# Order of the work inside a load, in a decode kernel with cached attention: the spread of P over two loads, its turn in the second, P V ahead of the second scores

## The chip, the cores and the metric

The kernel runs on one core of one Trainium2 chip. The metric is the device time of one execution in microseconds (us), taken as the median of several executions. The profile is one profiled execution on the same core.

## What is computed

One decode step (one new token for each of 8 rows) of a transformer layer: a layer norm, an attention over the last 2048 cached positions, and a mixer with a GELU MLP. Cut to what matters here:

```python
h  = x + A(layernorm(x), k_cache, v_cache, wq, wo)     # attention
h2 = h + B(layernorm(h), w1, w2, w3, w4)               # mixer, MLP

def A(x, k_cache, v_cache, wq, wo):   # 8 rows, 32 query heads, 8 KV heads, Dh = 128
    q = (x @ wq) ...                  # one query per row and head
    k, v = the last W = 2048 of the 8192 cached positions, each KV head shared by 4 heads
    p = softmax(q k^T / sqrt(Dh))
    return (p v) @ wo
```

With a sequence length of 1 the token shift of B leaves only zeros, so `w1` and `w2` are not read. What must be read is K and V (8 rows x 8 heads x 2048 x 128 in bf16, 33.6 MB each) and the weights wq, wo, w3 and w4: 79.18 MB in all.

## The kernel before, in words

**Loads.** K and V are read in 16 loads each, n = 0 to 15. A load holds 4 of the 8 KV heads of one batch row, 2 MiB, so a row b has two loads: the first (even n, in the code `t == 0`) and the second (odd n, `t == 1`). A load of K is worked on in four blocks (`i = 4n` to `4n + 3`). K and V have four buffers each. All large transfers are issued from one queue (SP) in program order: in step n of the loop K of load n, then V of load n - 3, and twice a piece of wo. K waits until K of load n - 4 has been turned, V until P V of four loads earlier is done. At the end V of load 15 comes in four pieces, then the rest of wo, then w3 and w4 into buffers of K.

**Program order.** Every engine has a list of operations written by hand; semaphores tie the lists. The order in which the Python functions are called is the order on each engine, and an engine never passes a waiting operation. The parts of a step:

- `turn_K(i)` (lines 298 to 311): TensorE (PE) transposes one block of K, 8 matmuls of 128x128 (L305), into one of two PSUM buffers `kT_ps`, used in turn; ScalarE (ACT) copies the low half of the result to SBUF (L292), VectorE (DVE) the high half (L293). The buffer is free again for the turn after the next when both copies are done.
- `pe_QK(m)` (L320): the scores of two turned blocks, 8 matmuls with 512 columns, summed in `S_ps`. `pe_QK(2n)` needs blocks 0 and 1 of the load, `pe_QK(2n+1)` blocks 2 and 3.
- `softmax_1`, `_2`, `_3` (second load of a row only): the maximum over the scores (DVE, L330), brought over partitions with a small matmul (L334), a reduction and a negation (DVE), brought back with another (L345), copied (DVE, L348); then the exponential on ACT (L351) into `P_sb`.
- `softmax_spread(b, part)`, part = 0 to 3: P is multiplied with a mask into the wide tile `Pz`, two DVE operations for each part (L366); part 0 also forms the masked row sums (L357).
- `softmax_4(b)`: `Pz` is turned like a block of K, 8 matmuls (L377) into the next `kT_ps`, and copied by ACT and DVE into `pS`, the weights of P V.
- `softmax_5(b)`: the row sums brought over partitions by a matmul into the small PSUM tile `sm` (L385), their reciprocals and a product (DVE, L388 and L394).
- `emit_PVs(k)`: P V in blocks (w = 0 to 3 of a load, 8 matmuls of 256 columns each, L421), three loads behind K (four in the last two steps); after the last block of a load ACT copies the result out (L430, `evict_o`).
- `fold_os` (matmuls L439, and a DVE product L445 into `oK`) and `turn_os` (matmuls L457, a DVE copy L462 into `o2`) finish a load of P V. L439, L457, L385, L334 and L345 all write the tile `sm`, one after the other.

**Order of a step before.** Both loads: turn 0, fold, turn 1, turn 2, first scores, `turn_os`, turn 3, one block of P V, second scores. In a first load the four parts of the spread of the row before lie between the turns, `softmax_5` stands ahead of turn 3, and `softmax_4` after the second scores, followed by three blocks of P V. In a second load `softmax_1` to `_3` follow the second scores, with a block of P V between each, and one behind them.

**After the loop**: the spread of the last row in one go (8 DVE operations), P V of load 12, `softmax_5` and `softmax_4` of the last row, P V of loads 13 to 15 in another form (L411, 16 matmuls a block), the projection with wo (`pe_wo`, L498), the layer norm, w3 (L631), GELU and w4 (L659), and the store.

Of the kernel before, what the change touches and what calls it, by code (L numbers as in the profile page):

```python
# [48 lines left out]
SPR = 4  # L49
# [32 lines left out]
def bass_sequential_preLN__sliding_block_cached__mixer_s_mlp__decode_kernel(  # L82
# [24 lines left out]
    with es:  # L107
# [178 lines left out]
        def turn(mm, dst, waits, waits_hi=(), free=()):  # L286
            k = len(e_Tlo)
            prev = lambda l: l[k - 2] if k >= 2 else None
            ps = kT_ps[k % 2]
            e_Tlo.append(PE.op(lambda e: mm(e, ps, 0), prev(e_lo), e_pk, e_pp, *waits))  # L290
            e_Thi.append(PE.op(lambda e: mm(e, ps, 1), prev(e_hi), *waits_hi))
            e_lo.append(AC.op(lambda e: e.activation(dst[:, 0:1024], ps[:, 0:1024], ACT.Copy), e_Tlo[k], *free))  # L292
            e_hi.append(DV.op(lambda e: e.tensor_single_scalar(dst[:, 1024:2048].bitcast(dt.int32),  # L293
                                                               ps[:, 1024:2048].bitcast(dt.int32), 0, ALU.bitwise_or),
                              e_Thi[k], *free))
            return e_Thi[k], (e_lo[k], e_hi[k])

        def turn_K(i):
            n, u = divmod(i, U)
            src = knat[:, n % NK, 2048 * u:2048 * (u + 1)].bitcast(dt.float32)  # L300

            def mm(e, ps, half):
                ps = ps[:, :].bitcast(dt.float32)
                for c in range(4 * half, 4 * half + 4):
                    ins = e.matmul(ps[:, c * 128:(c + 1) * 128], src[:, c * 128:(c + 1) * 128], perm_k[:, :],  # L305
                                   is_transpose=True)
                return ins
            e_T[i], e_ev[i] = turn(mm, kT_sb[:, i % NKT, :], ((sem_k[n % NK], 16 * (n // NK + 1)),),
                                   free=(e_QK.get((i - NKT) // 2),))

        def pe_QK(m):
            n, v = divmod(m, 2)
            b, t = divmod(n, NU)
            lo = 24 - 16 * t - 8 * v
            kT = kT_sb[:, (2 * m) % NKT:(2 * m) % NKT + 2, :].rearrange("p u (c j r k) -> p j k (u c) r", c=8, j=J, k=2)

            def f(e):
                for k in range(2):
                    for j in range(J):
                        ins = e.matmul(S_ps[b % 2][32 * j:32 * (j + 1), :].rearrange("p (c r) -> p c r", c=16),  # L320
                                       qz[:, b % 2, J * t + j, k, lo:lo + 32], kT[:, j, k],
                                       start=(t == 0 and v == 0 and k == 0), stop=(t == NU - 1 and v == 1 and k == 1),
                                       tile_position=(0, 32 * j), skip_group_check=True)
                return ins
            e_QK[m] = PE.op(f, *e_ev[2 * m], *e_ev[2 * m + 1], e_qw[b], e_qs, e_exp.get(b - 2))
# [29 lines left out]
        def softmax_spread(b, part):  # L355
            if part == 0:
                e_lsel[b] = DV.op(lambda e: e.tensor_scalar(lsel[:, :], sel_f[:, :], lcol[:, b % 2:b % 2 + 1], None,  # L357
                                                            ALU.mult), e_exp[b], e_Lb.get(b - 1), e_sel)
            w = 512 // SPR
            for a in range(w // 64):  # L360
                o = w * part + 64 * a
                p = P_sb[:, o:o + 64]
                p_bc = bass.AP(tensor=p.tensor, offset=p.offset, ap=[p.ap[0], [1, RR], [0, J], [RR, 2]])
                m = mJ[:, :]
                m_bc = bass.AP(tensor=m.tensor, offset=m.offset, ap=[m.ap[0], [0, RR], [1, J], [0, 2]])
                e_Pz[b, part] = DV.op(lambda e, o=o, p_bc=p_bc, m_bc=m_bc: e.tensor_tensor(  # L366
                    Pz[:, 0, J * o:J * (o + 64)].rearrange("p (x j k) -> p x j k", j=J, k=2), p_bc, m_bc, ALU.mult),
                    e_exp[b], e_PT.get(b - 1), e_mJ)

        def softmax_4(b):  # L370
            s = b % 2

            def mm(e, ps, half):
                ps = ps[:, :].bitcast(dt.float32)
                src = Pz[:, 0, :].bitcast(dt.float32)
                for c in range(4 * half, 4 * half + 4):
                    ins = e.matmul(ps[:, c * 128:(c + 1) * 128], src[:, c * 128:(c + 1) * 128], perm_p[:, :],  # L377
                                   is_transpose=True)
                return ins
            e_PT[b], e_pS[b] = turn(mm, pS[:, s, :], (e_Pz[b, SPR // 2 - 1],), (e_Pz[b, SPR - 1],),  # L380
                                    free=(e_PV.get(NU * U * (b - 1) - 1),))
            
        def softmax_5(b):
            s = b % 2
            e_Lb[b] = PE.op(lambda e: e.matmul(sm[:, LB], ones_f[:, :], lsel[:, :], start=True, stop=True),  # L385
                            e_lsel[b], sm_read[0])
            s = b % 2
            e_r = DV.op(lambda e: e.reciprocal(rL[:, s, :].rearrange("p (t j h) -> p t j h", t=NU, j=J),  # L388
                                               sm[:, LB].rearrange("p (j t h) -> p t j h", j=J, t=NU)), e_Lb[b],
                        e_sc.get(NU * (b - 2) + 1))  # L390
            sm_read[0] = e_r
            r_bc = bass.AP(tensor=rL[:, :, :].tensor, offset=s * H, ap=[rL[:, :, :].ap[0], [1, H], [0, R]])
            k_bc = bass.AP(tensor=mK[:, :].tensor, offset=0, ap=[mK[:, :].ap[0], [0, H], [1, R]])
            e_rL[b] = DV.op(lambda e: e.tensor_tensor(rLk[:, s, :, :], r_bc, k_bc, ALU.mult), e_r, e_mK)  # L394
# [56 lines left out]
        def turn_o(n):  # L451
            b, t = divmod(n, NU)
            dst = sm[:, 0:16]

            def f(e):
                for r in range(R):
                    ins = e.matmul(dst[32 * r:32 * (r + 1), :].rearrange("p (g k) -> p g k", k=R), mE[:, :],  # L457
                                   oK[:, n % 2, :, r, :], start=True, stop=True,
                                   tile_position=(0, 32 * r), skip_group_check=True)
                return ins  # L460
            e = PE.op(f, e_mE, e_sc[n], sm_read[0])
            e_scale[n] = DV.op(lambda e: e.tensor_copy(o2[:, J * t:J * (t + 1), :, b],  # L462
                                                       dst.rearrange("p (g k) -> p g k", k=R)), e)
            sm_read[0] = e_scale[n]
# [62 lines left out]
        def turn_os(to):  # L527
            while turned[0] < to:
                turn_o(turned[0])
                turned[0] += 1  # L530

        def emit_PVs(to):
            while pv[0] < min(to, NBLK):
                emit_PV(pv[0])
                pv[0] += 1

        for n in range(NUN):
            if n < NUN - 1:
                load_k(n)
            if n == NUN - 2:  # L540
                load_k(n + 1)
            if n >= LVD:
                load_v(n - LVD)
            if n in WO_AT:
                load_wo(WO_G[WO_AT.index(n)], sem_wo)
            i = U * n
            b, t = divmod(n, NU)
            lag = LVD + (n >= NUN - 2)
            pvs = lambda k: emit_PVs(U * (n - lag) + k)
            if t == 0 and b >= 1:  # L550
                spread = lambda part: softmax_spread(b - 1, part)
            else:
                spread = lambda part: None
            if t == 0:
                fill_q(b)
            turn_K(i)
            spread(0)
            fold_os(pv[0] // U)
            turn_K(i + 1)
            spread(1)  # L560
            turn_K(i + 2)
            spread(2)
            pe_QK(2 * n)
            turn_os(pv[0] // U)
            if t == 0 and b >= 1:
                softmax_5(b - 1)
            turn_K(i + 3)
            spread(3)
            pvs(1)
            pe_QK(2 * n + 1)  # L570
            if t == 0 and b >= 1:
                softmax_4(b - 1)
            if t == 1:
                softmax_1(b)
                pvs(2)
                softmax_2(b)
                pvs(3)
                softmax_3(b)
            pvs(4)
        for part in range(SPR):  # L580
# [127 lines left out]
```

## Time and profile before

| | |
|---|---|
| median of 3 runs | 200.86 us (199.88, 200.86, 203.51) |
| the profiled execution: its own time | 199.77 us |
| its span, first to last instruction | 198.5 us |
| PE busy, weight loads busy | 145.5 us, 112.6 us |
| DVE busy, ACT busy, POOL busy | 101.2 us, 89.5 us, 7.4 us |
| read from HBM | 79.18 MB |
| PE idle for K's transfer (L305) | 1.7 us in 2 waits (weight loads 3.2 us in 4) |
| PE idle for L462 ahead of L385 | 8.1 us in 6 waits |
| PE idle ahead of L320 for the copies of K | 10.2 us in 16 waits |

The clock is the one that the throttle granted to TensorE; 1.00 in a stretch means full speed and 0.50 half speed. "Idle before, released by" in a line of the profile names what ended the wait of that engine. Overlapping matmuls are counted once in a stretch's busy time.

### The profile page before, as it was taken

To read this page: it belongs to the slowest core of one execution; us is meant where nothing else is said; L and a number is where in the kernel's file an instruction comes from. 1 tells how busy PE (TensorE), PEld (TensorE's weight loads), DVE (VectorE), ACT (ScalarE), POOL (GpSimd) and SP (SyncE) were. 2 spreads that over 40 slices of the span, in tenths; PEclk is the share of its full clock that TensorE was granted. 3 is DMA by queue.
4 is the path that set the end of the run, shared out by engine and by line. 5 is a ranking of instruction groups with operands and counts; after the bars stand their busy time and mean duration, and the time that the engine had idled before them with its cause. 6 is when DMAs were issued, how large, how long until landed. Compare 5 with 4: busy or idle time off the path is not lost.

```text
span 198.5 us, 4498 instructions
## 1 busy us (share of the span) xinstructions
PE 145.5 (73%) x1987; PEld 112.6 (57%) x1987; DVE 101.2 (51%) x256; ACT 89.5 (45%) x113; POOL 7.4 (4%) x28
## 2 busy tenths in 40 slices
PE   0038985887969688967886879678959685786755
PEld 0037763673748465845664758456738563585744
DVE  5402454865665476548562765485627665530031
ACT  6001565864728274735572537354826382140022
POOL 5002001001000100010001000100000000000000
PEclk9999999999999999999998799999996999555555
DMA  6999999999999999999999999999999999999920
GB/s 239 429 426 426 429 426 429 426 431 426 423 417 432 423 429 418 423 429 436 410 435 426 426 423 426 429 419 424 439 429 426 419 423 429 395 411 406 391 107 2
DMA packets 7538, 79.46 MB, mean 400 GB/s; under 512 B 856, under 2 KB 864, under 8 KB 3424
## 3 DMA queue, kind: packets, MB, share of 16 engines
q1 hardware_dynamic: 7504, 79.18, 94.9%
q8 instruction: 15, 0.25, 0.5%
q14 instruction: 3, 0.02, 0.0%
q10 hardware_dynamic: 16, 0.01, 0.0%
HBM read 79.18 MB, written 0.01 MB: 399 GB/s over the span
## 4 chain that ended last, share of the span: by engine, by line
DMA 40%; PE 36%; DVE 18%; issue 3%; ACT 1%; SPq 0%; DVEq 0%
DMA knat<-in_A_k_cache_dram 40%; PE kT_ps L305 17%; DVE kT_sb L293 7%; DVE Pz L366 6%; PE S_ps L320 4%; PE oT_ps L411 3%; PE kT_ps L377 2%; PE S_ps L498 2%; DVE mcol L330 1%; PE sm L439 1%; PE oT_ps L421 1%; PE sm L385 1%; PE S_ps L659 1%; PE sm L345 1%; PE sm L334 1%
## 5 line engine op out<-in xcount | busy, mean ns | idle before, releaser
L292 ACT ACTIVATE kT_sb<-kT_ps 128x1024 bf16<-128x1024 bf16 x64 | 63.6, 1023 | 45.2 <-PE kT_ps L305 45.2
L305 PE MATMUL kT_ps<-perm_k,knat 128*128 128x128 f32 x512 | 70.2, 290 | 2.0 <-DMA knat<-in_A_k_cache_dram 1.7
L305 PEld LDWEIGHTS kT_ps<-perm_k,knat 128*128 128x128 f32 x512 | 61.6, 152 | 8.7 <-issue 4.9
L293 DVE TENSOR_SCALAR kT_sb<-kT_ps 128x512 int32<-128x512 int32 x64 | 44.2, 690 | 36.2 <-PE kT_ps L305 36.2
L320 PE MATMUL S_ps<-kT_sb,qz 128*32 128x512 bf16 x256 | 19.8, 383 | 10.4 <-DVE kT_sb L293 10.2
L366 DVE TENSOR_TENSOR Pz<-P_sb,mJ 128x256 bf16<-128x256 bf16 x64 | 23.8, 418 | 0.0
L421 PE MATMUL oT_ps<-vnat,pS 128*32 128x256 bf16 x416 | 20.6, 281 | 1.2 <-ACT oE L430 1.1
L351 ACT ACTIVATE P_sb<-S_ps,negcol 128x512 bf16<-128x512 f32 x8 | 5.5, 687 | 24.9 <-DVE negcol L348 24.9
L320 PEld LDWEIGHTS S_ps<-kT_sb,qz 128*32 128x32 bf16 x256 | 4.7, 94 | 17.4 <-ACT kT_sb L292 16.9
L292 ACT ACTIVATE pS<-kT_ps 128x1024 bf16<-128x1024 bf16 x8 | 8.2, 1023 | 12.0 <-PE kT_ps L377 12.0
L421 PEld LDWEIGHTS oT_ps<-vnat,pS 128*32 128x32 bf16 x416 | 9.5, 97 | 6.2 <-issue 4.0
L293 DVE TENSOR_SCALAR pS<-kT_ps 128x512 int32<-128x512 int32 x8 | 5.5, 692 | 9.2 <-PE kT_ps L377 9.2
L377 PE MATMUL kT_ps<-perm_p,Pz 128*128 128x128 f32 x64 | 9.6, 298 | 0.0
L377 PEld LDWEIGHTS kT_ps<-perm_p,Pz 128*128 128x128 f32 x64 | 7.7, 154 | 3.0 <-issue 3.0
L385 PE MATMUL sm<-lsel,ones_f 128*128 128x32 f32 x16 | 3.5, 303 | 8.1 <-DVE o L462 8.1
L259 PE MATMUL S_ps<-xlnT,wbig 128*128 128x8 bf16 x128 | 3.6, 168 | 7.7 <-DMA wbig<-in_A_wq_dram 7.7
L277 POOL COPY qz<-q_sb 64x64 bf16<-64x64 bf16 x16 | 4.6, 290 | 118.5 <-PE S_ps L320 102.6
L330 DVE TENSOR_REDUCE mcol<-S_ps 128x1 f32<-128x512 f32 x8 | 5.5, 692 | 6.5 <-PE S_ps L320 6.5
L439 PEld LDWEIGHTS sm<-selo,oE 128*128 128x128 f32 x52 | 8.1, 223 | 1.1 <-ACT oE L430 0.9
L385 PEld LDWEIGHTS sm<-lsel,ones_f 128*128 128x128 f32 x16 | 2.6, 203 | 10.7 <-DVE o L462 9.8
L439 PE MATMUL sm<-selo,oE 128*128 128x16 f32 x52 | 8.4, 277 | 0.0
L259 PEld LDWEIGHTS S_ps<-xlnT,wbig 128*128 128x128 bf16 x128 | 3.5, 104 | 7.8 <-issue 7.8
(90 smaller groups left out, 93.7 us busy)
## 6 DMA issues: line engine op xcount, KB each, us to landing
knat<-in_A_k_cache_dram SPq DMA_DIRECT2D x16, 2048.0 KB, 29.0
vnat<-in_A_v_cache_dram SPq DMA_DIRECT2D x15, 2048.0 KB, 30.9
wbig<-in_A_wq_dram SPq DMA_DIRECT2D x1, 4096.0 KB, 12.3
wbig<-in_A_wo_dram SPq DMA_DIRECT2D x2, 1024.0 KB, 31.1
vnat<-in_A_v_cache_dram SPq DMA_DIRECT2D x4, 512.0 KB, 8.2
wbig<-in_A_wo_dram SPq DMA_DIRECT2D x4, 512.0 KB, 10.0
knat<-in_B_w_dram SPq DMA_DIRECT2D x4, 448.0 KB, 12.0
knat<-in_B_w_dram SPq DMA_DIRECT2D x3, 512.0 KB, 15.3
```

The costliest lines, as they stand in the source:

```text
L259: ins = e.matmul(S_ps[0][:, h * B:(h + 1) * B], wq_v[:, kc, h * DH:(h + 1) * DH], xlnT[:, kc * B:(kc + 1) * B], start=(kc == 0), stop=(kc ...
L292: e_lo.append(AC.op(lambda e: e.activation(dst[:, 0:1024], ps[:, 0:1024], ACT.Copy), e_Tlo[k], *free))
L293: e_hi.append(DV.op(lambda e: e.tensor_single_scalar(dst[:, 1024:2048].bitcast(dt.int32), ps[:, 1024:2048].bitcast(dt.int32), 0, ALU.bitwi ...
L305: ins = e.matmul(ps[:, c * 128:(c + 1) * 128], src[:, c * 128:(c + 1) * 128], perm_k[:, :], is_transpose=True)
L320: ins = e.matmul(S_ps[b % 2][32 * j:32 * (j + 1), :].rearrange("p (c r) -> p c r", c=16), qz[:, b % 2, J * t + j, k, lo:lo + 32], kT[:, j, k],
L330: e_max[b] = DV.op(lambda e: e.tensor_reduce(mcol[:, :], S_ps[b % 2][:, :], AX.X, ALU.max), e_QK[4 * b + 3], e_mT.get(b - 1))
L366: e_Pz[b, part] = DV.op(lambda e, o=o, p_bc=p_bc, m_bc=m_bc: e.tensor_tensor(Pz[:, 0, J * o:J * (o + 64)].rearrange("p (x j k) -> p x j k" ...
L377: ins = e.matmul(ps[:, c * 128:(c + 1) * 128], src[:, c * 128:(c + 1) * 128], perm_p[:, :], is_transpose=True)
L385: e_Lb[b] = PE.op(lambda e: e.matmul(sm[:, LB], ones_f[:, :], lsel[:, :], start=True, stop=True), e_lsel[b], sm_read[0])
L411: ins = e.matmul(oT_ps[:, 0:16], vnat[:, n % NV, (16 * w + c) * DH:(16 * w + c + 1) * DH], pS[:, b % 2, o:o + 31:2], start=(w == 0 and c = ...
L421: ins = e.matmul(oT_ps[MO * q:MO * (q + 1), NO * (n % 2):NO * (n % 2 + 1)], pS[:, b % 2, o:o + 2 * MO - 1:2], vnat[:, n % NV, (16 * w + 2 ...
L439: ins = e.matmul(sm[:, 32:48], oE[:, o:o + 128], selo[:, 16 * s:16 * s + 16], start=(s == 0), stop=(s == 2 * VP - 1))
```

## The change

Only the order of the calls in a step of the loop changes; every operation is still issued once for each row or load, with the same operands. In the first load of a row the spread's parts 0 to 2 stay, each one place later (part 0 behind the second turn, part 1 behind the third, part 2 behind turn 3), and `softmax_5` goes behind the second scores. Part 3 of the spread goes into the second load of the row, behind its first turn, and `softmax_4` into the second load too, between the first scores and turn 3. In both loads `fold_os` goes from behind the first turn to ahead of the first scores, `turn_os` behind turn 3, and two blocks of P V instead of one stand ahead of the second scores. In the second load the rest of P V stands between the pieces of the softmax, none behind them.

```diff
             turn_K(i)
-            spread(0)
-            fold_os(pv[0] // U)
-            turn_K(i + 1)
-            spread(1)
-            turn_K(i + 2)
-            spread(2)
+            if t == 1 and b >= 1:
+                softmax_spread(b - 1, SPR - 1)
+            turn_K(i + 1)
+            if t == 0 and b >= 1:
+                softmax_spread(b - 1, 0)
+            turn_K(i + 2)
+            if t == 0 and b >= 1:
+                softmax_spread(b - 1, 1)
+            fold_os(pv[0] // U)
             pe_QK(2 * n)
+            if t == 1 and b >= 1:
+                softmax_4(b - 1)
+            turn_K(i + 3)
             turn_os(pv[0] // U)
             if t == 0 and b >= 1:
-                softmax_5(b - 1)
-            turn_K(i + 3)
-            spread(3)
-            pvs(1)
+                for part in range(2, SPR - 1):
+                    softmax_spread(b - 1, part)
+            pvs(2)
             pe_QK(2 * n + 1)
-            if t == 0 and b >= 1:
-                softmax_4(b - 1)
-            if t == 1:
+            if t == 0:
+                if b >= 1:
+                    softmax_5(b - 1)
+            else:
                 softmax_1(b)
-                pvs(2)
+                pvs(3)
                 softmax_2(b)
-                pvs(3)
+                pvs(4)
                 softmax_3(b)
             pvs(4)
```

More of the change, by code (lines that the diff above doesn't have):

```diff
@@ L549, in bass_sequential_preLN__sliding_block_cached__mixer_s_mlp__decode_kernel @@
             pvs = lambda k: emit_PVs(U * (n - lag) + k)
-            if t == 0 and b >= 1:
-                spread = lambda part: softmax_spread(b - 1, part)
-            else:
-                spread = lambda part: None
             if t == 0:
@@ L556, in bass_sequential_preLN__sliding_block_cached__mixer_s_mlp__decode_kernel @@
             turn_K(i)
-            spread(0)
+            if t == 1 and b >= 1:
[6 more added lines that the diff above has]
+                softmax_spread(b - 1, 1)
             fold_os(pv[0] // U)
-            turn_K(i + 1)
-            spread(1)
-            turn_K(i + 2)
-            spread(2)
             pe_QK(2 * n)
+            if t == 1 and b >= 1:
+                softmax_4(b - 1)
+            turn_K(i + 3)
             turn_os(pv[0] // U)
             if t == 0 and b >= 1:
-                softmax_5(b - 1)
-            turn_K(i + 3)
-            spread(3)
-            pvs(1)
+                for part in range(2, SPR - 1):
+                    softmax_spread(b - 1, part)
+            pvs(2)
             pe_QK(2 * n + 1)
-            if t == 0 and b >= 1:
-                softmax_4(b - 1)
-            if t == 1:
+            if t == 0:
+                if b >= 1:
+                    softmax_5(b - 1)
+            else:
                 softmax_1(b)
-                pvs(2)
+                pvs(3)
                 softmax_2(b)
-                pvs(3)
+                pvs(4)
                 softmax_3(b)
```

## The prediction

> **What bounds the kernel now.** First the 40 slices of the page: clock, DMA share, rate.
>
> ```profile
> PEclk9999999999999999999998799999996999555555
> DMA  6999999999999999999999999999999999999920
> GB/s 239 429 426 426 429 426 429 426 431 426 423 417 432 423 429 418 423 429 436 410 435 426 426 423 426 429 419 424 439 429 426 419 423 429 395 411 406 391 107 2
> ```
>
> The transfers run without a gap to about 189 us: 79.18 MB at 426 GB/s are 186 us. They set when a load of K is there; a load of K and one of V (4.19 MB) take 9.85 us. Issue to landing is 29.0 us for K by the table of DMA issues, so an issue that moves by a few us moves no landing. Next, busy time per load in mid-kernel; columns: stretch, length, busy time (instructions) of PE, weight loads, DVE, ACT, POOL, then clock, DMA share, GB/s.
>
> ```profile
> 79.39:88.21 8.82, 7.30 (x97) 5.35 (x93) 4.50 (x11) 4.41 (x6) 0.58 (x2) 1.00 1.02 433
> 88.21:98.26 10.05, 8.11 (x103) 6.06 (x99) 6.99 (x18) 5.91 (x8) 0.00 (x0) 1.00 0.99 420
> 138.21:148.15 9.94, 7.45 (x93) 5.35 (x93) 4.47 (x10) 5.42 (x8) 0.00 (x0) 1.00 1.01 429
> 148.15:158.37 10.22, 8.24 (x67) 7.04 (x67) 6.42 (x17) 4.33 (x5) 0.00 (x0) 0.83 1.00 425
> 158.37:167.91 9.54, 6.93 (x87) 4.77 (x85) 5.19 (x11) 5.61 (x8) 0.00 (x0) 1.00 1.02 435
> ```
>
> Undisturbed, a second load takes 8.82 us and a first 10.05: 18.87 a row, against 19.70 of transfers. So work follows transfers, with 0.83 us of slack a row. The last three rows are loads 13, 14 and 15. The chain of waits ends its last stretch of DMA here:
>
> ```profile
> 116.05 32.05 DMA knat<-in_A_k_cache_dram
> 148.10 0.04 issue
> 148.15 1.24 PE kT_ps L305 x8
> ```
>
> From the landing of K of load 14 at 148.10 to the end everything is compute. K of load 15 was issued right behind it, so it lands one load (4.92 us) later, 153.0, and isn't waited for. The timeline of PE (start, duration, idle before with its releaser) shows the waits:
>
> ```profile
> 154.70 0.41 PE L385 MATMUL sm<-lsel,ones_f 128*128 128x32 f32 x2 [1.10 <-DVE o L462]
> 156.89 0.62 PE L320 MATMUL S_ps<-kT_sb,qz 128*32 128x512 bf16 x8 [0.88 <-DVE kT_sb L293]
> ...
> 163.69 0.62 PE L320 MATMUL S_ps<-kT_sb,qz 128*32 128x512 bf16 x8 [0.54 <-DVE kT_sb L293]
> ...
> 170.63 0.20 PE L457 MATMUL sm<-oK,mE 128*32 128x16 bf16 x4 [1.44 <-DVE oK L445]
> ...
> 183.53 0.62 PE L498 MATMUL S_ps<-o,wbig 128*128 128x8 bf16 x17 [1.00 <-issue]
> ...
> 189.77 0.30 PE L498 MATMUL S_ps<-o,wbig 128*128 128x8 bf16 x6 [1.69 <-issue]
> ```
>
> The DMA shares by single microseconds fade out by 192, when w4 must be there; its first matmuls run at 194.47 and its last at 196.1. So compute from 148 on could shrink by some 4 us before w4 sets the end. That, and not the row, is what the change can be worth.
>
> **The change, first load.** Out: the turn of P, 1.02 us and 0.44 us of idle ahead of it (load 8). Out: the stall of L385, 1.40 us in mid-kernel, 1.10 in load 14; L385 waits for `o2`, queued on DVE behind two spread products (0.75 us) and a copy of K. It now stands behind the second scores, when `o2` is about 0.9 us old. Out where P V exists: 0.40 us, a second block of P V (0.40) in the 0.54 us wait of the second scores. In: the first turn follows L345 directly, and its copy on ACT queues behind the exponential (0.69 + 0.19 us); bound 0 to 0.5, I take 0.4, since the copy now starts 0.9 us after the turn and could start after 0.6. The moved `fold_os` costs nothing: result copied out long before, DVE product due only behind turn 3. Sum: 10.05 - 1.46 - 1.40 - 0.40 + 0.4 = 7.2. PE's own busy time, less the turn, is 7.1, which leaves no gap; I take 7.6 (7.1 to 7.9).
>
> **Second load.** In: the turn of P, 1.02 us. It stands ahead of turn 3 and so of the P V and the second scores queued there; its two copies (1.02 on ACT, 0.69 on DVE) run under turn 3 (0.92), so the first P V of this row, which needs them, waits 0 to 0.3. In: two products of the spread (0.67) on DVE ahead of the copies of blocks 1 and 2: the first scores wait 0 to 0.5, I take 0.1, since DVE is idle 4.3 of 8.82 us here. Out: 0.40 as above. Sum 8.82 + 1.02 + 0.1 - 0.4 = 9.5 (9.4 to 9.9). The blocks of P V between the softmax pieces stay one and one. V arrives one transfer after its K: in load 13 P V waited 0.38 us for V (the weight loads' row at 143.24). Second scores behind two blocks inherit that: nothing in a second load, where P V now comes about 1 us later, up to 0.8 in a first; loads 14 and 15 don't meet it (load 14 has no P V; V of load 11 lands near 158, is used near 161). No step passes a DMA issue on SP; V of load 15, issued after P V of load 11, moves earlier under 6 us of queued transfers. POOL's copies of q wait for the same scores.
>
> A row is then 17.1 us, and the 1.8 us saved turn into waiting for K. The order of landings decides where: a first load is done 2.2 us before the next K, and a second load, 9.5 of 9.85, can't make up a late start.
>
> **The end, load by load.** The clock comes in. PE waited 1.05 us for K of load 14, and stretches of the profile give the clock:
>
> ```profile
> 145.57:148.98 3.41, 1.96 (x28) 1.38 (x21) 0.65 (x3) 1.19 (x4) 0.00 (x0) 1.00 1.05 447
> 148.98:152.39 3.41, 3.41 (x19) 3.41 (x18) 2.15 (x6) 1.91 (x2) 0.00 (x0) 0.50 0.98 418
> ```
>
> After a wait of 0.65 us (at 107.84) and of 1.05 us, the clock was 0.50 for 3.4 us, and two turns took 3.14 us instead of 1.94; a load loses 1.3 us (load 10: 11.39 against 10.05). [...]
>
> Load 13: K lands at 138.2 (issued 103.18, 35.0 us). PE will have waited some 2 us, so half clock: 9.5 + 1.3, done at 149.0; before it was done at 147.1 and waited. Load 14 then has no wait and full clock: 10.22, less the turn of P and its idle (0.9, as load 15's first turn followed it directly), less the stall 1.10, less 1.4 of half clock = 6.8, done at 155.8 instead of 158.37. Load 15 to its second scores was 163.69 - 158.37 = 5.3; with the turn of P 1.02, DVE's spread 0.2, P V in the wait -0.1: 6.4, so at 162.2. Gain 1.5; from there to the exponential nothing changes (max, two small matmuls, a P V between each). Behind it PE's idle of 1.09 us (P V waiting for L430, now copied out before the exponential) is removed but worth nothing: L457 waits for `oK` on DVE, behind all eight products of the spread, as before. So the rest shifts as a whole: w3 and w4 are there in time, and clock is 0.50 either way. I take 1.3 off, between the schedule's 1.5 and the 0.7 left if DVE's and ACT's bounds above come in full.
>
> The profiled execution took 199.77 (span 198.5, 1.3 around it): 198.5. The median lies 1.09 above it: 199.6. Two of the three runs lie within that step, so 199.5.
>
> **The rivals.**
> 1. *Full clock everywhere* (waits for K too short, or falling so that no window empties): load 13 is done at 147.7, load 14 starts at 148.1, load 15's second scores come at 161.3: 2.4 off, 198.5. For: the windows at 125 and 84 had gaps of up to 0.6 us and stayed at 1.00. Against: the expected wait is 2 us.
> 2. *Second loads become the bound, slower.* The turn of P makes every second load the long one, it starts late because of K, at half clock, and if the clock drops again in load 14 or 15, the slack is gone: load 13 done at 149.4 (9.9 + 1.3), load 14 8.2, load 15 6.9 + 1.3 to its second scores: 165.8, 2.1 later, 203.0. Decides: a half-clock stretch after 149. For: clock falls easily in this kernel. Against: PE has no gap over 0.6 us in loads 14 and 15 as scheduled. With one such drop: +0.8, 201.7.
> 3. *Hidden*: the gain in load 14 is spent by load 13's late end and DVE's copies: 200.9. For: load 13 ends 1.9 later by my own sum, and errors of 0.3 us a load add up.
> 4. *Code arrives late elsewhere.* The stalls of 1.00 and 1.69 us in L498 have no releaser, and 127 matmuls lie between them; packets of the instruction queue run just ahead of them. If waits in PE's list grow or shrink by more than the 6 matmuls left there, the second falls into w3's 56 matmuls, partly hidden: up to 1.7 more off, 197.8. [...]
>
> **How the numbers follow.** Forecast 0.45, rival 1 0.15, rival 2 0.15, rival 3 0.17, rival 4 0.08. Range: from rivals 1 and 4, less the median's excess of 1.09 (197.4 and lower) to rival 2 (203.0): 197.2 to 202.8 leaves out about 2 in 10. Two per cent, about what a measurement can tell from no change, is 196.8 or 204.9: faster needs rivals 1 and 4 together, 0.05; slower needs more than two drops, 0.06; within, 0.89.
>
> **What would show it.** Right: PE waits about 2 us for K of odd loads, not of load 14; load 14 takes near 6.8 at clock 1.00; L385's wait for L462 (8.1 us in 6) is gone; load 15's second scores near 162; L457 still waits for L445. Wrong: half clock in loads 14 or 15, first scores of second loads waiting over 0.5 for DVE, P V waiting for `pS` or V, PE idle for K at load 14 above 1 us, or another length of the stretch from the last exponential to the end.

## The result and the profile after

The median fell from 200.23 us (22 runs, 198.35 to 203.51) to 198.25 us (22 runs, 196.68 to 200.09); the ratio is 0.9914, 95% interval 0.9889 to 0.9940, so 1.2 to 2.2 us faster: a change within two per cent, to which the prediction gave 0.89. The ratio leaves out executions more than 1.5% above the fastest of their kernel, the medians do not. The profiled execution took 198.7 us (span 197.4), 1.07 under that of before.

The page of the changed kernel, clock and transfers in 40 slices:

```profile
PEclk9999999999999998899999799969699999655555
DMA  6999999999999999999999999999999999999940
```

The transfers are as they were, without a gap. The busy time per load (columns as in the prediction): the first two lines are loads 8 and 9 in mid-kernel, the last three are loads 13, 14 and 15, the last of them up to the exponential.

```profile
86.81:94.25 7.44, 7.06 (x91) 5.18 (x90) 5.67 (x16) 4.54 (x6) 0.00 (x0) 1.00 1.01 427
95.50:105.00 9.50, 8.17 (x100) 6.34 (x100) 5.43 (x13) 5.18 (x6) 0.58 (x2) 1.00 1.01 419
...
138.37:149.27 10.90, 9.67 (x100) 8.00 (x101) 5.57 (x12) 5.39 (x6) 0.00 (x0) 0.84 1.00 425
149.27:156.01 6.74, 5.90 (x60) 4.56 (x59) 5.20 (x14) 4.55 (x6) 0.00 (x0) 1.00 1.01 430
156.01:165.67 9.66, 7.98 (x103) 5.88 (x102) 5.94 (x13) 5.21 (x7) 0.00 (x0) 1.00 1.01 427
```

A first load lost 2.6 us (10.05 to 7.44), a second one gained 0.7 (8.82 to 9.50). Load 13 now has the half clock (0.84 over the load, 0.50 from 138.48 to 141.89), load 14 full clock (1.00); of its waits only that of the second scores is left (0.75 us, 0.88 before). In the timeline of PE:

```profile
138.37 4.51 PE L305 MATMUL kT_ps<-perm_k,knat 128*128 128x128 f32 x24 [2.13 <-DMA knat<-in_A_k_cache_dram]
...
155.21 0.62 PE L320 MATMUL S_ps<-kT_sb,qz 128*32 128x512 bf16 x8 [0.75 <-DVE o L462]
155.76 0.41 PE L385 MATMUL sm<-lsel,ones_f 128*128 128x32 f32 x2
...
162.61 0.62 PE L320 MATMUL S_ps<-kT_sb,qz 128*32 128x512 bf16 x8 [0.32 <-DVE kT_sb L293]
...
169.55 0.20 PE L457 MATMUL sm<-oK,mE 128*32 128x16 bf16 x4 [2.93 <-DVE oK L445]
...
188.69 0.30 PE L498 MATMUL S_ps<-o,wbig 128*128 128x8 bf16 x6 [1.70 <-issue]
```

PE waits 2.13 us for K of load 13; L385 has no wait any more; the second scores of load 15 start at 162.61 instead of 163.69. From there to the end it takes 34.8 us in both kernels (197.4 - 162.6, 198.5 - 163.7). So in the profiled executions the whole difference, 1.08 us, arises between the landing of K of load 14 and those scores: load 14 starts 1.1 us later (149.27, before 148.15), takes 3.5 less, and load 15 takes 1.3 more up to its second scores.

### The profile page after: what moved, and what is told of

It reads as the page before. It is cut to its first block, busy times and chain, and to the rows that moved or that the text cites. A ratio compares the mean times of both kernels' runs of the same rounds, so it can differ in the third digit from the quotient of the medians.

```text
span 197.4 us, 4498 instructions
## 1 busy us (share of the span) xinstructions
PE 146.9 (74%) x1987; PEld 116.8 (59%) x1987; DVE 100.0 (51%) x256; ACT 89.3 (45%) x113; POOL 7.4 (4%) x28
## 4 chain that ended last, share of the span: by engine, by line
DMA 44%; PE 37%; DVE 12%; issue 3%; ACT 3%; SPq 0%; DVEq 0%
DMA knat<-in_A_k_cache_dram 44%; PE kT_ps L305 16%; PE S_ps L320 5%; DVE kT_sb L293 5%; PE kT_ps L377 3%; PE oT_ps L411 3%; DVE Pz L366 3%; PE S_ps L498 2%; DVE mcol L330 1%; PE sm L439 1%; ACT P_sb L351 1%; ACT kT_sb L292 1%; PE S_ps L661 1%; PE sm L385 1%; PE oT_ps L421 1%
## 5 line engine op out<-in xcount | busy, mean ns | idle before, releaser
L305 PE MATMUL kT_ps<-perm_k,knat 128*128 128x128 f32 x512 | 72.4, 300 | 10.2 <-DMA knat<-in_A_k_cache_dram 9.7
L305 PEld LDWEIGHTS kT_ps<-perm_k,knat 128*128 128x128 f32 x512 | 64.1, 155 | 18.0 <-DMA knat<-in_A_k_cache_dram 11.6
L293 DVE TENSOR_SCALAR kT_sb<-kT_ps 128x512 int32<-128x512 int32 x64 | 43.7, 689 | 37.1 <-PE kT_ps L305 37.1
L421 PE MATMUL oT_ps<-vnat,pS 128*32 128x256 bf16 x416 | 19.2, 279 | 0.0
L430 ACT ACTIVATE oE<-oT_ps 128x256 f32<-128x256 f32 x13 | 5.0, 384 | 29.3 <-PE oT_ps L421 29.3
L421 PEld LDWEIGHTS oT_ps<-vnat,pS 128*32 128x32 bf16 x416 | 10.3, 96 | 2.3 <-issue 0.4
L439 PEld LDWEIGHTS sm<-selo,oE 128*128 128x128 f32 x52 | 7.5, 209 | 0.2 <-DVE negcol L348 0.2
L439 PE MATMUL sm<-selo,oE 128*128 128x16 f32 x52 | 7.5, 259 | 0.0
```

The lines of the kernel that those rows point to most:

```text
L421: ins = e.matmul(oT_ps[MO * q:MO * (q + 1), NO * (n % 2):NO * (n % 2 + 1)], pS[:, b % 2, o:o + 2 * MO - 1:2], vnat[:, n % NV, (16 * w + 2 ...
L439: ins = e.matmul(sm[:, 32:48], oE[:, o:o + 128], selo[:, 16 * s:16 * s + 16], start=(s == 0), stop=(s == 2 * VP - 1))
```

## The experiments

The theory: loads 0 to 13 only have to keep up with the transfers, and the stall of L385 in load 14, with the clock there, is what the change takes off the end. Rivals: the turn of P in the second load carries the gain; the time saved in each row does; something behind load 15 does. Each run is compared with the kernel before on the same chip.

**1. The late sum alone**, in the kernel before.

```diff
             turn_os(pv[0] // U)
-            if t == 0 and b >= 1:
-                softmax_5(b - 1)
             turn_K(i + 3)
...
             pe_QK(2 * n + 1)
             if t == 0 and b >= 1:
+                softmax_5(b - 1)
                 softmax_4(b - 1)
```

> The kernel before with one edit: softmax_5 of a first load behind its second scores (ahead of the turn of P). Theory (compute from the landing of K of load 14 sets the end; the stall of L385 was the waste in a first load): the wait of L385 for L462 (8.1 us in 6) falls under 1 us; a first load takes 8.7 instead of 10.05, so PE waits for K of odd loads and load 13, not load 14, gets the half clock; load 14 takes 7.7 at clock 1.00 instead of 10.22, second scores of load 15 start near 161.4 instead of 163.69. Time 2.3 us under before (ratio 0.989), so at least as much as the whole change. Rival (the turn of P in the second load is what gains): under 0.5 us of gain, ratio 0.998 to 1.000.

Ratio 0.9895 (0.9840 to 0.9951), median 197.69 us: this one move is worth about as much as the whole change (0.9914; the two intervals overlap), and the rival falls. A step was wrong: load 13 kept its full clock (1.00 from 138.19 to 148.20), was done early, and K of load 14 was waited for, as before, with the clock drop in load 14 (0.81 from 148.20 to 157.41). The timeline of PE in this kernel:

```profile
138.19 1.09 PE L305 MATMUL kT_ps<-perm_k,knat 128*128 128x128 f32 x8 [1.44 <-DMA knat<-in_A_k_cache_dram]
...
148.20 1.73 PE L305 MATMUL kT_ps<-perm_k,knat 128*128 128x128 f32 x8 [1.12 <-DMA knat<-in_A_k_cache_dram]
...
162.74 0.62 PE L320 MATMUL S_ps<-kT_sb,qz 128*32 128x512 bf16 x8 [0.54 <-DVE kT_sb L293]
```

Its second scores came at 162.74, not 161.4. In this execution the wait of 1.44 us cost load 13 no clock, and that of 1.12 us was followed by the 0.81 of load 14.

**2. The turn of P in the second load alone**, in the kernel before.

```diff
             spread(0)
+            if t == 1 and b >= 1:
+                softmax_spread(b - 1, SPR - 1)
...
             pe_QK(2 * n)
+            if t == 1 and b >= 1:
+                softmax_4(b - 1)
...
-            spread(3)
...
-            if t == 0 and b >= 1:
-                softmax_4(b - 1)
```

> The kernel before with one edit: part 3 of the spread and the turn of P (softmax_4) in the second load, as in the change; softmax_5, fold and P V stay. Theory: a first load gets 1.4 us shorter, a second 1.0 longer; load 13 starts late for K at half clock and ends near 149.4; load 14 takes 7.9 (stall of 1.1 still there) at clock 1.00; load 15 needs 6.5 to its second scores, near 163.8 against 163.69: no gain, ratio 1.000 (0.996 to 1.004). Rival (this part carries the gain): ratio 0.99.

Ratio 1.0017 (0.9952 to 1.0082): no gain, as expected. The median of its 12 executions, 203.36 us, lies 2.2 above that of the kernel before on this chip (201.17); its profiled execution, one of 204.48 us, had a clock drop in five rows in succession (0.6 to 0.7 in five slices of its page; more below).

**3. The new order in the last row only, and everywhere but there** (the second run has the opposite condition, `n < NUN - NU`).

```diff
             if t == 0:
                 fill_q(b)
+            if n >= NUN - NU:
+                turn_K(i)
+                if t == 1 and b >= 1:
+                    softmax_spread(b - 1, SPR - 1)
...
+            else:
                 turn_K(i)
                 spread(0)
...
```

> The new order in loads 14 and 15 alone, the order of before in loads 0 to 13. Theory: loads up to 13 only have to keep up with the transfers, so most of the gain stays: load 13 ends near 147.1, PE waits 1 us for K of load 14, load 14 runs at half clock for 3.4 us and takes 8.2, second scores of load 15 near 162.7; time 1.0 us under before, ratio 0.995. Rival (the 1.8 us saved in each row count): no gain, ratio 1.000.

> The new order in loads 0 to 13, the order of before in loads 14 and 15 (the opposite of the last-row run). Theory: load 13 ends near 149 after a half-clock stretch, load 14 runs at full clock but with the stall and the turn of P, 8.8 us; second scores of load 15 near 163.2, 0.5 us ahead of before: ratio 0.996 to 0.999. Rival (the time saved per row counts): ratio 0.992 or lower.

Ratio 0.9925 (0.9874 to 0.9976) for the last row only, 1.0033 (0.9986 to 1.0080) for all rows but the last. The gain sits in the last two loads; what is saved in the 14 before is waited away. The first run's ratio is below the 0.995 expected, which its interval still holds; its profiled execution had the clock drop in load 12 (0.5 and 0.8 in the page's slices from 127.7 to 137.5), no wait for K of load 14 and full clock in it (1.00 from 148.47 to 155.09), and the second scores of load 15 at 161.70 instead of 162.7. In the second run load 13 is that of the changed kernel, 10.90 us at clock 0.84 (138.35 to 149.25). Its load 14, busy time:

```profile
149.25:158.41 9.16, 6.66 (x67) 5.42 (x67) 6.48 (x18) 4.86 (x7) 0.00 (x0) 1.00 1.00 424
```

The late end of load 13 (1.1 us after K of load 14) uses up what the full clock saves in load 14: 9.16 us instead of the 10.22 before, 1.06 less. The second scores of load 15 came at 163.73, where before has 163.69; the 0.5 us expected weren't there.

**4. Two blocks of P V ahead of the second scores, alone**, in the kernel before.

```diff
-            pvs(1)
+            pvs(2)
             pe_QK(2 * n + 1)
...
-                pvs(2)
+                pvs(3)
                 softmax_2(b)
-                pvs(3)
+                pvs(4)
                 softmax_3(b)
```

> The kernel before with one edit: two blocks of P V instead of one ahead of the second scores (the rest one block earlier each). Theory: it shortens each load by 0.4 us of the scores' wait, but loads 0 to 13 are paced by transfers, load 14 has no P V, and load 15 gets 0.1; the exponential no longer delays the copy L430 after it, which is hidden: gain 0.1 us, ratio 0.998 to 1.002. Rival (work per load counts everywhere): 0.4 us in each of 13 loads, ratio 0.98 or lower.

Ratio 1.0012 (0.9970 to 1.0054). The wait of the second scores is shorter (0.32 instead of 0.54 us), and no time comes of it; that it is hidden under the transfers fits run 3, but this run alone doesn't show it.

**5. The change without its late sum.**

```diff
+            turn_os(pv[0] // U)
+            if t == 0 and b >= 1:
+                softmax_5(b - 1)
             turn_K(i + 3)
-            turn_os(pv[0] // U)
...
-            if t == 0:
-                if b >= 1:
-                    softmax_5(b - 1)
-            else:
+            if t == 1:
```

> The changed kernel with softmax_5 (and turn_os ahead of it) back in front of the turn of block 3; all the rest of the change stays. Theory: the stall of L385 for L462 is back, about 1.1 us in load 14, so second scores of load 15 move from 162.6 to 163.7 and most of the gain is lost: ratio 0.996 to 1.000. Rival (the other parts carry the gain): ratio 0.990 to 0.993, as the change.

Ratio 1.0040 (0.9999 to 1.0082): all of the gain is gone. `turn_os` goes back together with the sum, so the run returns both. PE's timeline shows the wait of load 14 back, split over two instructions since the fold is late now, and its second scores at half clock (1.05 us instead of 0.62):

```profile
154.47 0.19 PE L457 MATMUL sm<-oK,mE 128*32 128x16 bf16 x4 [0.93 <-DVE oK L445]
155.00 0.41 PE L385 MATMUL sm<-lsel,ones_f 128*128 128x32 f32 x2 [0.34 <-DVE o L462]
...
157.19 1.05 PE L320 MATMUL S_ps<-kT_sb,qz 128*32 128x512 bf16 x8 [0.88 <-DVE kT_sb L293]
```

The second scores of load 15 came at 165.67, 2.0 later than expected: the stall came back, and with it a clock drop behind it (0.92 over load 14, 0.90 from there to 168.70).

**6. PE's idle time filled: the clock.** First, in the kernel before, matmuls on constants in the waits of the softmax, to see whether the clock follows PE's idle time. A ratio of 0.990 to 0.993 was expected, with no half clock ahead of load 15's end.

```diff
                 softmax_1(b)
                 pvs(2)
+                fill(8)
                 softmax_2(b)
                 pvs(3)
+                fill(4)
                 softmax_3(b)
```

> The kernel before with idle PE filled: in a second load 8 matmuls of 128x128 on constants (bf16, about 0.5 us, result never read) ahead of L334 and 4 ahead of L345, where PE waits 0.57 and 0.40 us for DVE. No other edit; it only adds work. [...] Rival (the clock follows something else, or added work costs time): ratio 1.000 to 1.005 and the same spread.

Ratio 0.9928 (0.9886 to 0.9970), median 198.55, none over 200.43. The number came as expected and the reason did not: this execution had half clock in load 14 (second scores of 1.04 us instead of 0.62, at 156.71), and its second scores of load 15 started at 165.08, 1.4 later than before. The gain came after them, 32.3 us to the end instead of 34.8. Both long stalls in the projection had left it:

```profile
182.50 1.86 PE L498 MATMUL S_ps<-o,wbig 128*128 128x8 bf16 x64
...
185.11 1.05 PE L411 MATMUL oT_ps<-pS,vnat 128*128 128x16 bf16 x33 [0.34 <-issue]
```

The filling had added 96 matmuls to PE's list, 192 instructions (4,498 to 4,690), and that moved the places of the stalls (run 7). So the clock was tried again, in the changed kernel: 24 matmuls ahead of the first turn of loads 7, 9, 11 and 13, where PE waits for K (2.13 us at load 13), and 32 small ones ahead of the projection with wq, together a shift of 256 instructions, close to the 254 that lie between the two stalls:

```diff
+            if t == 1 and 7 <= n < NUN - 1:
+                fill(24)
             turn_K(i)
```

> [...] Theory of the clock: PE is busy in the wait, the half-clock stretch at the start of load 13 goes, load 13 takes 9.6 instead of 10.9 and ends near 148, second scores of load 15 start 0.9 to 1.3 us earlier than 162.6; ratio to before 0.984 to 0.988. Rival (the clock doesn't set the end, or the added work delays load 13): ratio 0.990 to 0.994.

Ratio 0.9882 (0.9823 to 0.9941), between the two expectations. The stalls in the projection stayed (0.73 and 1.70 us). Loads 13 and 14:

```profile
138.34:148.12 9.78, 8.17 (x101) 6.35 (x100) 5.55 (x13) 5.32 (x7) 0.00 (x0) 1.00 1.01 427
148.12:156.22 8.10, 7.41 (x58) 6.23 (x59) 5.00 (x13) 4.74 (x6) 0.00 (x0) 0.79 1.01 429
```

Load 13 lost its half clock and 1.1 us (9.78 against 10.90), load 14 got it (0.79 against 1.00): second scores of load 15 at 162.83, no gain in this execution. PE was early at K of load 14, and the drop only moved.

**7. The shift of the list alone.** 96 small matmuls ahead of the projection with wq, in both kernels. In the kernel before, both stalls were expected to leave L498, for a ratio of 0.987 to 0.990.

```diff
+        def pe_pad(e):
+            for _ in range(96):
+                ins = e.matmul(S_ps[1][:, 0:32], ident_b[:, :], ident_b[:, 0:32], start=True, stop=True)
+            return ins
+        PE.op(pe_pad, e_idb)
         e_q = PE.op(pe_q, e_xT, (sem_wq, 16))
```

> The kernel before with 96 small matmuls on constants (128x32 bf16, result never read) added once, ahead of the projection with wq, where PE waits 7.7 us for wq. They shift every later place in PE's list by 192 instructions and touch nothing else. [...] Rival (the stalls belong to the wo transfers or to L498 itself): stalls stay, ratio 1.000.

> The changed kernel with the same 96 matmuls at the same place. Theory: the two gains add, since neither has reached w4's landing near 192 (L661, the matmuls with w4, would start near 190.9 instead of 193.4, its last block of w4 is needed about 1.5 us later): time 3.7 to 4.3 us under before, ratio 0.979 to 0.982. Rival (w4 sets the end): at least 1 us of it lost, ratio 0.984 or more.

In the kernel before: 0.9964 (0.9925 to 1.0003), less than expected and not clear of no change. Both stalls left L498 and 0.61 us came elsewhere; from the second scores of load 15 to the end it took 32.5 us, 2.3 less. But those scores came at 166.19, because two first loads ran into half clock. Stretches of this execution:

```profile
134.05:137.46 3.41, 1.73 (x22) 1.31 (x26) 2.65 (x8) 1.02 (x1) 0.00 (x0) 1.00 1.02 430
137.46:140.87 3.41, 3.41 (x32) 2.08 (x35) 0.96 (x3) 1.02 (x1) 0.00 (x0) 0.50 0.99 423
...
154.53:157.94 3.41, 1.46 (x14) 1.23 (x18) 2.65 (x9) 1.02 (x1) 0.00 (x0) 1.00 0.98 418
157.94:161.35 3.41, 3.41 (x21) 2.65 (x14) 1.02 (x3) 1.02 (x1) 0.00 (x0) 0.50 1.03 437
```

The 3.41 us ahead of each drop hold 1.1 of the 1.40 us of the stall of L385 (its line is 390 here) and the wait of the second scores (0.54 and 0.88): PE is busy 1.73 and 1.46 us of them. No wait for K is near. So half clock came here behind the stall that the change removes, and such a load took 11.6 us (129.69 to 141.29), against 10.05 without a drop.

In the changed kernel: 0.9838 (0.9779 to 0.9896), median 196.54, between the two expectations. Loads 13 and 14 ran at full clock here, second scores at 161.54, and w4 began to bind: its matmuls (L661, here L666) waited 0.16 us for it. From those scores to the end it took 33.2 us, 1.6 less than without the 96 matmuls.

A row of the DMA view bears on these stalls. The queue `q8 instruction` moves 15 packets, 0.25 MB, in the whole execution of before and of the changed kernel, and one of them goes 2.5 to 2.7 us ahead of the end of each stall: in the kernel before at 180.98 and 187.11 (stalls end at 183.53 and 189.77), in the changed one at 179.89 and 186.19 (182.45 and 188.69). That code comes late there is an estimate from these times and from the places that moved; what the time between is spent on isn't shown.

**8. A version better than both.** The changed kernel, the 96 matmuls, and two moves at the end. The first was also run alone:

```diff
+        fold_os(NUN - 4)
         for part in range(SPR):
             softmax_spread(NB - 1, part)
...
-        softmax_5(NB - 1)
         softmax_4(NB - 1)
+        softmax_5(NB - 1)
```

> The changed kernel with one edit: the fold of P V of load 11 (L439, and L445 on DVE) is issued ahead of the spread of the last row instead of behind it. In the changed kernel L457 waits 2.93 us for L445, which is queued behind eight products of the spread; its input is there at 165.1, ahead of the exponential. Theory: that wait goes to under 1 us, P V of load 12 runs beside the spread, the turn of P starts near 168.5 to 169.4 instead of 171.0; time 1.6 to 2.3 us under the changed kernel, ratio to before 0.980 to 0.984. Rival (w4 or the late code set the end): under 0.5 us more than the change, ratio 0.989 to 0.992.

> The changed kernel with three edits: the 96 matmuls, the fold of load 11 ahead of the last spread, and at the end the turn of P (softmax_4) ahead of softmax_5, so that it no longer waits for L462. Theory: 2.5 us for the code, 1.0 for the fold as its profile showed, 0.5 to 1.0 for the turn, of which w4's landing leaves little beyond the first two: it ends 2.9 to 4.0 us under the changed kernel's span of 197.4, w4 being waited for; ratio to before 0.970 to 0.978. Rival (w4 is reached sooner): as the changed kernel with the 96 matmuls alone, 0.979 to 0.982.

The fold alone: 0.9890 (0.9831 to 0.9949), in the range of the rival. In its profiled execution it took 33.9 us from the second scores of load 15 (162.47) to the end, 0.9 less than in the changed kernel, where 1.6 to 2.3 were expected. L457 waits no more, but L385 now waits for the copy behind it, which is queued after the same eight products:

```profile
166.58 0.18 PE L457 MATMUL sm<-oK,mE 128*32 128x16 bf16 x4
...
169.48 0.64 PE L385 MATMUL sm<-lsel,ones_f 128*128 128x32 f32 x2 [2.02 <-DVE o L462]
```

All three edits: 0.9797 (0.9750 to 0.9843), median 196.12, 195.85 to 196.23, the lowest median of all, and a miss of the expected 0.970 to 0.978; it lies in the range of the rival. It isn't told apart from the padded change alone: the profiled executions span 194.8 and 194.7 us, and both take 33.2 us from the second scores of load 15. Its profile shows why there isn't more:

```profile
187.71 1.98 PE L639 MATMUL kT_ps<-Pz,knat 128*128 128x8 bf16 x56 [0.98 <-DMA knat<-in_B_w_dram]
...
191.48 1.00 PE L667 MATMUL S_ps<-Pz,knat 128*128 128x8 bf16 x24 [0.18 <-DMA knat<-in_B_w_dram]
```

L639 is here the matmul with w3, L667 with w4. Both weights are waited for: the transfers now set the end (47 GB/s from 191 to 192 us, none behind), and compute is done 3 us behind them.

## Why the prediction was right, and where it was off

- *Transfers pace the loop, and the end starts at K of load 14*: right; the order of before in the last row loses the gain (1.0033), the new order there alone has it (0.9925).
- *Loads*: first 7.44 (7.6 forecast), second 9.50 (9.5), load 13 10.90 (10.8), load 14 6.74 (6.8), load 15 to its second scores 6.60 (6.4). The scores at 162.61 against 162.2: load 13 began 0.2 late and took 0.1 longer, and DVE's spread ahead of the copies cost 0.37 us of wait at load 15's first scores, where 0.2 was taken.
- *The wait for K moves to odd loads and takes the half clock with it*: right in the profiled execution (2.13 us and clock 0.84 at load 13). It isn't fixed: other executions have the drop in load 14 (0.81 in run 1, 0.79 in run 6) or in neither load (1.00 in both, run 7). That the schedule met this execution to 0.4 us is in part luck.
- *L457 still waits for L445; the rest shifts as a whole*: right, 2.93 us, and 34.8 us to the end in both.
- *The forecast's size*: 199.5 forecast, 198.25 measured. The term that was mis-sized is the median's place against the profiled execution: "The median lies 1.09 above it: 199.6", of which 1.0 went into the 199.5. It came from three executions. Over 22, the median of before lies 0.46 above its profiled execution (199.77), that of the changed kernel 0.45 below its own (198.70). The profiled execution itself was 0.2 over the forecast 198.5. So I took the profiled execution of before as more typical than it is. It had no clock drop behind L385; runs 5, 6 and 7 show such drops in kernels that keep that stall, in first loads and with no wait for K near (second scores of 1.05, 1.04 and 1.04 us instead of 0.62). By an estimate from the 11.6 us of such a load against 10.05, the stall can so cost more than its own 1.1 us. The fall is 1.07 us between the profiled executions, 1.98 between the medians and 1.7 by the ratio; how much of the difference is due to such drops isn't settled, since each kernel has one profile.
- *The parts*: I spread the worth over the turn's leaving, the stall and the clock. The late sum alone does as much as the whole (0.9895), the rest without it gains nothing (1.0040). The sum for the whole was right, because the turn's 0.9 us off load 14 comes back as 1.0 in load 15, as the working had it.
- *Rivals*: the full clock of rival 1 is what the padded change showed in loads 13 and 14 (1.00 in both; second scores of load 15 at 161.54, 161.3 forecast). Its windows are stretches of 3.41 us like those of the prediction's rows, and that one must be part empty for the clock to fall was an estimate from these rows; ahead of the drops listed below PE was busy 0.38 to 2.05 us of such a stretch, and once 1.92 us left the clock at 1.00. The stalls put down to late code, given 0.08, didn't move with this change (1.00 and 1.70 us remain), but 96 matmuls ahead of them move them, and in the profiled execution took 2.3 us off the end of the kernel before (run 7). No run shows late code as their cause, nor the 2.5 us "for the code" in the sum of run 8; what the runs showed for the 96 matmuls is 2.3 us between the second scores of load 15 and the end of the kernel before, with a ratio of 0.9964, and 1.6 us there in the changed kernel.

## What to carry to other kernels

Where transfers pace a loop, cost an edit at the place where the pacing ends: here two loads out of sixteen decide, and a stall there counts, while the same stall earlier is waited away. A small matmul that waits for a neighbour engine's backlog is best issued after that backlog, not ahead of the large work. Before believing a filler or a reorder, look whether it moved stalls that have no releaser; in run 6, 192 instructions that compute nothing made the kernel before faster for another reason than the one they were put in for.

## What the runs showed of the hardware

- In the profiles of before and after, half clock ahead of the last exponential came for 3.41 us at a time: 148.97 to 152.38 in the kernel before and 138.48 to 141.89 in the changed one, at 0.50, with 1.00 ahead and behind. In the 3.41 us ahead of a drop PE was busy 1.74 and 1.96 us in the kernel before (drops at 108.0 and 148.97), 1.37, 0.38, 2.05 and 1.29 in the changed one (77.03, 107.75, 128.23 and 138.48), 1.73 and 1.46 in the padded kernel of before (137.46 and 157.94). Busy time alone isn't the condition: of the stretches in step with the drops, 1.92 us in the kernel before (84.13 to 87.54) was followed by full clock. What decides stays open.
- The drops recurred row by row in some executions. In run 2's profiled execution the page has the clock at 0.6 to 0.7 in slices 16, 20, 24, 28 and 32, four slices of 5.07 us or 20.3 us apart, and the first loads of two of the rows there start at 110.84 and 131.33, 20.5 apart. Run 6 (filling in the softmax) has half-speed second scores (1.04 us instead of 0.62) at 136.43 and 156.71, 20.3 apart, the padded kernel of before drops at 137.46 and 157.94, 20.5 apart. A row of 18.87 us with a drop of some 1.5 (11.6 us against 10.05 for the load) is nearly that long; why it settles there, and doesn't in other executions, isn't shown.
- In a dense part of its list PE stood still for 1.00 and 1.70 us with no releaser, 127 matmuls (254 instructions) apart, with the transfers at some 400 GB/s during the first and fading during the second (239 GB/s from 188 to 190 us in the kernel before); 192 more instructions ahead of them moved their places (run 7), 256 more left them in the projection, 0.73 and 1.70 us (run 6). The rows of the engines don't say why; that code came late is an estimate from the moved places and from the packets of the instruction queue, 2.5 to 2.7 us ahead of each stall's end in the kernels before and after.
